# Sliding-window attention and MLP, two layers on one core: score tiles of 64 keys, and the output product of two head groups in one burst

## The chip, the cores and the metric

The kernel runs on one core of a Trainium2 chip. The metric is the device time of one execution in microseconds (us), the median of several. A profile of one execution gives the start and length of every instruction on the five engines: TensorE (PE; its weight loads are listed apart, as PEld), VectorE (DVE), ScalarE (ACT), GpSimd (POOL) and SyncE (SP), which here only issues transfers.

## What is computed

Two layers over 2048 tokens of width 576; each is attention in a sliding window, then an MLP, both after a layer norm and added to the input:

```python
def _A_ref(x, wqkv, wo):
    B, S, D = x.shape
    H = 32; Dh = D // H; W = 256
    qkv = (x @ wqkv).reshape(B, S, 3, H, Dh).transpose(2, 0, 3, 1, 4)
    q, k, v = qkv[0], qkv[1], qkv[2]
    scores = einsum("bhqd,bhkd->bhqk", q, k) * (Dh ** -0.5)
    mask = (idx[:, None] - idx[None, :] >= 0) & (idx[:, None] - idx[None, :] < W)
    p = softmax(where(mask, scores, -1e9))
    o = einsum("bhqk,bhkd->bhqd", p, v)
    return o.transpose(0, 2, 1, 3).reshape(B, S, D) @ wo

def _B_ref(x, w1, b1, w2, b2):
    h = gelu(einsum("bsd,df->bsf", layernorm(x), w1) + b1)      # 576 -> 4608
    return einsum("bsf,fd->bsd", h, w2) + b2                    # 4608 -> 576

for layer in range(2):          # the same weights in both
    x = x + _A_ref(layernorm(x), A_wqkv, A_wo)
    x = x + _B_ref(layernorm(x), B_w1, B_b1, B_w2, B_b2)
```

32 heads have 18 elements each. A query sees itself and the 255 keys before it, so a block of 128 keys is seen by three blocks of 128 queries: its own (where the upper triangle is masked), the next (all of it), and the one after (where the other triangle is masked).

## The kernel before

**Who sets the order.** Python code describes every piece of work as a task with its engine, what it reads and writes, a cost and a priority (`Plan.add`, L206). `Plan.schedule` (L257) plays these through engine by engine and always takes the task that can start first, ties by priority; it also assigns the eight PSUM banks, and puts dummy matmuls (`warm_fn`, L604) into planned gaps of TensorE in the first 140 us. The order so found is written out, one in-order stream an engine, and `Sched.add` (L65) puts in the semaphore waits. TensorE never waits for its own earlier work there (L75, L82). `PL.nudge` (L463) is a table of numbers that are added to the priorities of named stages; `FEED_UNTIL` (L418) is the time until which the planner holds TensorE work back that would make ACT run dry.

**How the work is cut.** Tokens stand in 16 tiles of 128 a layer, four tiles to a chunk: eight chunks, k = 0 to 7, of which 0 and 4 start a layer. Heads stand in eight groups of four. The main loop (L1032) mixes, for every k, the attention of chunk k (`E`, L858), the MLP of chunk k-1 (`G_part` for the first product and gelu, `mm2` for the second), the projections of chunk k+1 (`qkv`, L718), and the output projection with residual and layer norm (`tail`, L886).

**Attention of one group.** The four heads of a group lie on the partitions 0, 32, 64, 96. `scores` (L777) has keys on the output partitions: the matmul at L789 takes 32 rows (one head's dimensions, padded) and 128 keys, so the array works as four tiles of 32x128 side by side, one for a head. The 128-key blocks of a chunk are packed into three units (`units_of`, L765); in an inner chunk each has 512 columns of queries, in the first chunk of a layer 384, 512 and 256. A unit fills two pairs of PSUM banks (`SC`). ACT takes the exponential of each pair into `pT` (L798), and POOL sets the masked triangles to zero with an affine select over all 128 partitions (L819). `pv` (L824) multiplies by the values: tiles of 128x32, four heads side by side, 18 value columns and a one that gives the softmax sum (L834), all three units of a group in one burst of 24 matmuls into one bank, one unit behind the last scores. DVE transposes the result, divides by the sum, and transposes again for the output projection (L845 to L855).

**The MLP.** `G_part` adds the last 64 of the 576 rows for six column blocks at once, in two tiles of 64x128 (L919), which takes six banks; then four matmuls of 128 rows each (L931), gelu on ACT (L934). `mm2` has 288 columns a matmul (L960) and takes a bank of `FILL` (7, 6, 5, 4). Score and MLP banks overlap (`SC` uses 0 to 5, `MM1` all).

**The start.** SP loads the token tiles into `x_in` (the buffer of `w2`), ACT's queue loads the qkv weights (`w_load`, L573), then ACT loads its table of functions (L988). DVE clears the four upper banks (L601), computes statistics and normalizes; the first four tiles are transposed by TensorE (L657).

**Layer norm in the tail.** The last 64 columns of a normalized tile are written twice (for the two 64-row tiles), the second time by a second DVE instruction (L648, `dup`); SP then issues a transposing transfer (L663).

## Time and profile before

| | |
|---|---|
| median of three runs | 895.23 us (895.12 to 896.53) |
| the profiled execution | 897.23 us, its span 895.5 us |
| first matmul | 9.13 us |
| score matmuls L789, units | 1216, 192 |
| output product L834, bursts | 1408, 64 |
| exp L798 | 384 instructions, 345.8 us busy on ACT |
| masks L819 | 368 instructions, 283.5 us busy on POOL |
| mm2 L960, L931, qkv and output projection L699 | 2304, 1152, 1280 matmuls |

"x" with a number is a count of instructions. Names stand as output<-input with shapes as partitions x elements. In a timeline, equal instructions in a row are merged: the first number is their start, the second the time from the first start to the last end. A bracket tells how long the engine was idle before and what ended that. A matmul's record is longer than the time that it occupies the array: the next one starts while it still drains.

### The profile page before, as it was taken

What the parts mean: (1) busy time and instruction counts of PE and PEld (TensorE: products, weight loads), DVE (VectorE), ACT (ScalarE), POOL (GpSimd) and SP (SyncE); (2) the same over time, 40 slices, a digit from 0 to 9 for tenths busy, and PEclk for the clock granted to TensorE, in tenths of its full rate; (3) what the DMA queues carried; (4) which work ended last, traced back from release to release, by engine and by line L of the source; (5) the groups of instructions that cost most, each with busy time, mean ns of one, the idle gap of its engine ahead of it and who ended that gap; (6) DMA issues with size and microseconds to landing.
All of it is one profiled execution on the core that took longest, in us unless ns stands there. A gap on an engine that the chain in (4) does not pass through costs nothing.

```text
span 895.5 us, 19577 instructions
## 1 busy us (share of the span) xinstructions
PE 864.4 (97%) x7849; PEld 506.5 (57%) x7901; DVE 410.1 (46%) x969; ACT 615.8 (69%) x737; POOL 366.2 (41%) x504
## 2 busy tenths in 40 slices
PE   5898999999999999999999999999999999999998
PEld 4555455656566565665655655556556545556665
DVE  6789223863357351763427633375134523161111
ACT  3976888577767788366773868747777689844443
POOL 3677544274244662224431544416444266231100
PEclk9999999999999999999999999999999999999999
DMA  6788537742477333853457342682537632446431
GB/s 177 139 172 173 179 119 182 178 109 81 149 166 158 120 120 98 183 124 121 130 119 181 71 158 86 143 198 67 165 119 147 184 125 71 144 126 176 153 96 50
DMA packets 182649, 122.25 MB, mean 137 GB/s; under 512 B 107424, under 2 KB 181024, under 8 KB 182560
## 3 DMA queue, kind: packets, MB, share of 16 engines
q1 hardware_dynamic: 179152, 115.47, 49.5%
q0 software_dynamic: 1584, 3.54, 1.5%
q10 hardware_dynamic: 1824, 1.99, 0.7%
q8 instruction: 63, 1.03, 0.5%
q14 instruction: 26, 0.21, 0.1%
HBM read 91.28 MB, written 2.36 MB: 105 GB/s over the span
## 4 chain that ended last, share of the span: by engine, by line
PE 54%; DVE 1%; issue 1%; DMA 1%; ACT 1%; POOL 0%
PE ps L960 21%; PE ps L931 18%; PE ps L699 6%; PE ps L789 3%; PE ps L919 3%; PE ps L834 3%; ACT pT L798 1%; DVE x_res L880 0%; DMA xnTa<-xn 0%; DVE st_all L620 0%; DMA xnTm<-xn 0%; DVE xn L643 0%; DVE xn L648 0%; POOL rstd L633 0%; DVE xn L883 0%
## 5 line engine op out<-in xcount | busy, mean ns | idle before, releaser
L819 POOL TENSOR_SCALAR_AFFINE_SELECT pT<-pT 128x512 bf16<-128x512 bf16 (+1 forms) x368 | 283.5, 794 | 266.6 <-ACT pT L798 262.0
L798 ACT ACTIVATE pT<-ps 128x1024 bf16<-128x1024 f32 (+2 forms) x384 | 345.8, 972 | 58.3 <-PE ps L789 57.8
L934 ACT ACTIVATE hT<-ps,b1col 128x512 bf16<-128x512 f32 x288 | 197.8, 687 | 192.8 <-PE ps L931 188.3
L960 PE MATMUL ps<-w_sb,hT 128*128 128x288 bf16 x2304 | 309.5, 287 | 0.2
L960 PEld LDWEIGHTS ps<-w_sb,hT 128*128 128x128 bf16 x2304 | 213.9, 98 | 81.9 <-issue 24.9
L931 PE MATMUL ps<-xnTm,w_sb 128*128 128x512 bf16 x1100 | 255.0, 380 | 4.9 <-issue 3.2
L931 PEld LDWEIGHTS ps<-xnTm,w_sb 128*128 128x128 bf16 x1152 | 109.6, 98 | 137.0 <-issue 19.1
L880 DVE TENSOR_TENSOR x_res<-ps,x_res 128x288 f32<-128x288 f32 x216 | 95.9, 448 | 169.0 <-PE ps L960 158.4
L699 PE MATMUL ps<-wqkv,xnTa 128*128 128x288 bf16 x960 | 136.0, 289 | 3.5 <-DVE qn L742 1.9
L845 DVE STREAM_TRANSPOSE oq<-ps 128x512 f32<-128x512 f32 x64 | 45.8, 715 | 179.0 <-PE ps L834 178.8
L699 PEld LDWEIGHTS ps<-wqkv,xnTa 128*128 128x128 bf16 x960 | 88.4, 98 | 41.4 <-issue 7.8
L742 DVE CAST qn<-ps 128x288 bf16<-128x288 f32 x120 | 53.2, 449 | 35.1 <-PE ps L699 33.0
L942 POOL TENSOR_TENSOR x_res<-x_res,b2bc 128x576 f32<-128x576 f32 x32 | 40.8, 1274 | 69.2 <-ACT hT L934 69.2
L789 PE MATMUL ps<-qT,kT 32*128 32x384 bf16 (+2 forms) x1216 | 64.1, 276 | 2.2 <-ACT pT L798 2.0
L631 POOL TENSOR_SCALAR vtmp<-mv_all 128x1 f32<-128x1 f32 (+1 forms) x43 | 8.5, 197 | 121.4 <-DVE mv_all L622 120.6
L834 PE MATMUL ps<-pT,vA 128*20 128x384 bf16 (+2 forms) x1408 | 50.7, 276 | 2.0 <-ACT pT L798 0.9
L620 DVE BATCH_NORM_STATS2 st_all<-x_res 128x6 f32<-128x288 f32 x104 | 44.8, 448 | 1.2
L919 PE MATMUL ps<-xnTm,w_sb 64*128 64x512 bf16 x288 | 39.7, 381 | 5.5 <-ACT pT L798 3.3
L789 PEld LDWEIGHTS ps<-qT,kT 32*128 32x128 bf16 x1216 | 19.5, 92 | 44.1 <-issue 25.1
L699 PE MATMUL ps<-wo_sb,attT 128*128 128x288 bf16 x320 | 42.8, 286 | 0.1
L834 PEld LDWEIGHTS ps<-pT,vA 128*20 128x20 bf16 x1408 | 25.7, 90 | 26.8 <-issue 13.4
L729 DVE CAST vA<-ps 128x288 bf16<-128x288 f32 x64 | 28.8, 454 | 23.7 <-PE ps L699 23.4
(47 smaller groups left out, 347.6 us busy)
## 6 DMA issues: line engine op xcount, KB each, us to landing
w_sb<-in_B_w_dram SPq DMA_DIRECT2D x48, 864.0 KB, 5.4
w_sb<-in_B_w_dram SPq DMA_DIRECT2D x48, 768.0 KB, 4.7
w_sb<-in_B_w_dram SPq DMA_DIRECT2D x96, 48.0 KB, 4.4
x_res<-in_A_x_dram POOLq DMA_DIRECT2D x3, 1152.0 KB, 7.0
out_dram<-xn SPq DMA_DIRECT2D x16, 144.0 KB, 1.8
wqkv<-in_A_wqkv_dram ACTq DMA_DIRECT2D x3, 576.0 KB, 6.9
w_sb<-in_A_x_dram SPq DMA_DIRECT2D x2, 576.0 KB, 4.2
wo_sb<-in_A_wo_dram SPq DMA_DIRECT2D x4, 144.0 KB, 2.6
```

Source lines behind the costliest of these rows:

```text
L699: ins = e.matmul(bank(bs[o])[:, 0:HB], lhs(c), rhs(c, o * HB), start=(c == 0), stop=(c == KD - 1))
L742: add("dve", lambda e, b=bs[o], dst=dst: e.tensor_copy(dst, heads_of(bank(b))), reads=[bs[o]], writes=[f"qn{sl}h{o}"], cost=0.375, lat=0.1 ...
L789: ins = e.matmul(two(bs[j // 2])[:, j % 2, col:col + nq * 128], k_of(T0 + so)[0][32 * j:32 * j + 32, g, :], qs[32 * j:32 * j + 32, g, qo * ...
L798: add("act", lambda e, h2=h2: e.activation(pT[:, sl, 2 * h2:2 * h2 + 2, lo:hi], two(bs[h2])[:, :, lo:hi], ACT.Exp, scale=SCALE), reads=[bs ...
L819: add("pool", lambda e, ap=ap, pat=pat, sgn=sgn, kind=kind: e.affine_select(ap, ap, pattern=pat, compare_op=(ALU.is_ge if kind == "d" else ...
L834: ins = e.matmul(bank(bo)[32 * j:32 * j + VW, qo * 128:(qo + nq) * 128], vA[:, (T0 + so) % VS, 8 * j + g, :], pT[:, sl, j, col:col + nq * ...
L845: add("dve", lambda e: e.transpose(oq[:, 0:4 * nt, :].rearrange("p b c -> p (b c)"), bank(bo)[:, 0:nt * 128]), reads=[bo, f"aq{(g - 1) % G ...
L880: add("dve", lambda e: e.tensor_tensor(x_res[:, t, sl], bank(b)[:, 0:HB], x_old[:, t, sl], ALU.add), reads=[b] + ([f"xin{t}"] if first els ...
L919: ins = e.matmul(bank(bk)[:, 0:n], w1_sb[64 * b:64 * b + 64, sl, col:col + 128], xnTm[64 * b:64 * b + 64, k % 2, 4, 0:n], start=True, stop ...
L931: ins = e.matmul(bank(bk)[:, 0:n], w1_sb[:, sl, col:col + 128], xnTm[:, k % 2, c, 0:n], start=False, stop=(c == 3))
L934: add("act", lambda e, ff=ff, fl=fl, bk=bk: e.activation(hT[:, fl, 0:n], bank(bk)[:, 0:n], ACT.Gelu_apprx_tanh, bias=b1col[:, ff:ff + 1]), ...
L960: ins = e.matmul(bank(b)[:, 0:HB], hT[:, fl, i * 128:(i + 1) * 128], w2_sb[:, fl, hh * HB:(hh + 1) * HB], start=(fl == 0), stop=(fl == NFH ...
```

## The change

1. **Score tiles of 64 keys.** A block of 128 keys is scored as two halves of 64 (tiles of 32x64, eight side by side). For each half only the 320 queries that see any of its keys are computed, not 384, and the columns start at the half's first query. Units have 512, 320 and 448 columns in an inner chunk, and 320, 448 and 256 in a layer's first. `pT` becomes three buffers of unit kind 0, three of kind 1 and two of kind 2.
2. **Masks.** Blocks are 64 queries wide. POOL masks the diagonals of the lower half (64 partitions), of the upper half (128 partitions), and the far edge of the lower half; the far edge of the upper half is a minimum with a constant mask on DVE, which is made at the start.
3. **Output product.** `pv` takes two groups at once, each with its own bank, in tiles of 64x32: in phase 0 the upper keys of the second group run beside the lower keys of the first, in phase 1 the other way round. Phase 1 waits for the semaphore of phase 0 (`own=True`). There are 32 bursts of two phases.
4. **The start.** The table load of ACT stands ahead of its weight transfers. The four upper banks are cleared by TensorE with dummy matmuls (`clear`), not by DVE; more dummy matmuls fit in before the first tile. The load of tiles 8 to 11 waits for `q2`, not `k3`; `b1in` lies in `hT`.
5. **The rest.** The second copy of the last 64 columns goes from DVE to POOL; five buffers `qn`, not six; other bank choices for some tasks; `FEED_UNTIL` is 0; finer stage names in chunks 0, 1 and 7 (`FINE`), and a new table of nudges. `DRV = -1` and `DRQ = 0` leave the split between ACT and DVE as it was.

```diff
-            if lw is not None and not (eng == "pe" and lw[2] == "pe"):
+            if lw is not None and (own or not (eng == "pe" and lw[2] == "pe")):
...
-FEED_UNTIL = 40.0
+FEED_UNTIL = 0.0
...
-    PS = 6
-    PVG = [()] * 8
-    PVLAG = 1
+    PR = (3, 3, 2)
+    UW = (512, 320, 448)
+    LAG = 2
...
-    NQN = 6
+    NQN = 5
...
+    add("act", lambda e: e.preload_act_table_set("exp_and_others"), cost=1.4, lat=0.0, fifo="act", plain=True, prio=-10)
     w_load(0)
...
-    for i in OUT:
-        b = Bank((i,))
-        add("dve", lambda e, b=b: e.memset(bank(b), 0.0), writes=[b], cost=0.56, lat=0.1, prio=-7, alloc=[b])
...
+    add("dve", lambda e: e.tensor_copy(mk[64:128, :], unit(0, 0)[64:128, 0, 64:128]), reads=["p0_0m0"], writes=["mask"], cost=0.09, prio=-7)
...
+    for i in OUT:
+        b = Bank((i,))
+
+        def clear(e, b=b):
+            for h in range(2):
+                ins = e.matmul(bank(b)[:, 256 * h:256 * h + 256], warm[:, 0:128], warm[:, :], start=True, stop=True)
+            return ins
+        add("pe", clear, reads=["warm"], writes=[b], cost=0.45, lat=0.2, prio=-7, alloc=[b])
...
         if dup:
-            add("dve", lambda e: e.tensor_scalar(xn[:, sl, D:KD * 128], s[:, t, 512:D], mv_all[:, t, 0:1], rstd[:, t:t + 1],
-                                                  op0=ALU.subtract, op1=ALU.mult),
+            add("pool", lambda e: e.tensor_copy(xn[:, sl, D:KD * 128], xn[:, sl, 512:D]), reads=[f"xn{sl}"], writes=[f"xd{sl}"], cost=0.33,
...
         if nt == 4:
-            us = [[(0, 0, 3, 0), (-2, 0, 1, 384)], [(1, 1, 3, 128), (3, 3, 1, 0)], [(-1, 0, 2, 0), (2, 2, 2, 256)]]
+            us = [(1, [0]), (2, [1, 3]), (0, [2])] if t0 == 0 else [(0, [0, -2, 3]), (1, [1]), (2, [-1, 2])]
...
+                for b in range(2):
+                    lo = 128 * max(so, 0) + (64 * b if so >= 0 else 0)
+                    hi = 128 * min(so + 3, nt) - (64 * (1 - b) if so + 3 <= nt else 0)
+                    pad = 64 * b if even else 0
+                    halves.append((lo, hi, at[b] + pad, pad))
+                    at[b] += hi - lo + pad
...
-                    ins = e.matmul(two(bs[j // 2])[:, j % 2, col:col + nq * 128], k_of(T0 + so)[0][32 * j:32 * j + 32, g, :],
-                                   qs[32 * j:32 * j + 32, g, qo * 128:(qo + nq) * 128], start=True, stop=True, tile_position=(32 * j, 0))
+                        ins = e.matmul(two(bs[j // 2])[64 * b:64 * b + 64, j % 2, col:col + hi - lo],
+                                       k_of(T0 + so)[0][32 * j:32 * j + 32, g, 64 * b:64 * b + 64],
+                                       qs[32 * j:32 * j + 32, g, lo:hi], start=True, stop=True, tile_position=(32 * j, 64 * b))
...
+                add("dve", lambda e, ap=ap, mo=mo: e.tensor_tensor(ap, ap, mo, ALU.min),
+                    reads=[f"p{sl}h0", f"p{sl}h1", "mask"], writes=[f"p{sl}m{mi}"], cost=0.06 + 0.27 * nb, lat=0.14, prio=prio)
...
+        def fn(e, ph):
+            ins = None
+            at = [0, 0]
+            got = []
+            for b, i in ((1, 1 - ph), (0, ph)):
+                for x in half(i, b):
+                    got.append((at[b], len(got), x))
+                    at[b] += x[4] - x[3]
+            seq = [x[2] for x in sorted(got, key=lambda x: x[:2])]
...
+                    ins = e.matmul(bank(bo[i])[32 * j:32 * j + VW, lo:hi], vA[64 * b:64 * b + 64, (T0 + so) % VS, 8 * j + gs[i], :],
+                                   pu[64 * b:64 * b + 64, j, col:col + hi - lo], start=(ph == 0 and i not in begun),
+                                   stop=(ph == 1 and not any(x[0] == i for x in seq[n + 1:])), tile_position=(64 * b, 32 * j), skip_group_check=True)
...
+        for ph in range(2):
+            ncol = max(sum(x[4] - x[3] for x in half(ph, 0)), sum(x[4] - x[3] for x in half(1 - ph, 1)))
+            add("pe", lambda e, ph=ph: fn(e, ph), reads=rd, writes=bo, cost=0.02 + 0.1 * ph + ncol * 0.000425, prio=prio - 0.1 * ph, lat=0.2, mode="c",
+                alloc=(bo if ph == 0 else ()), fifo="pv", own=(ph == 1))
...
-    table("exp", -10)
...
-    xin_load(8, 4, ["k3"], -4)
+    xin_load(8, 4, [GX], -4)
```

## The prediction

> **What bounds the kernel now.** I read the page's busy times and its chain first, then a table by stages, then the timeline of one attention stage and of the first 18 us, and last the groups by shape.
>
> ```profile
> PE 864.4 (97%) x7849; PEld 506.5 (57%) x7901; DVE 410.1 (46%) x969; ACT 615.8 (69%) x737; POOL 366.2 (41%) x504
> ...
> PE 54%; DVE 1%; issue 1%; DMA 1%; ACT 1%; POOL 0%
> ```
>
> TensorE is busy for 97% of the span, and the chain that ended last names hardly anything but TensorE lines. So a change is worth what it takes from TensorE's stream, unless some stage has another limit. The stages show two that have (columns: stretch, its length, then busy us of PE, PEld, DVE, ACT and POOL, granted clock, DMA):
>
> ```profile
> 22.00:50.00 28.00, 24.48 (x281) 13.90 (x281) 22.72 (x59) 25.50 (x37) 19.27 (x27) 1.00 0.79 150
> 50.00:80.00 30.00, 29.53 (x342) 18.51 (x342) 26.22 (x60) 20.85 (x26) 20.13 (x30) 1.00 0.94 198
> 80.00:92.00 12.00, 9.34 (x114) 5.26 (x106) 11.84 (x29) 9.74 (x11) 10.08 (x15) 1.00 0.37 72
> ...
> 600.00:716.00 116.00, 115.47 (x1087) 67.82 (x1095) 48.17 (x110) 85.95 (x99) 48.11 (x64) 1.00 0.52 137
> 716.00:745.00 29.00, 26.80 (x257) 13.44 (x262) 7.71 (x16) 24.01 (x29) 16.05 (x19) 0.94 0.41 129
> 745.00:806.00 61.00, 57.82 (x554) 32.69 (x558) 25.48 (x61) 45.09 (x53) 26.23 (x38) 1.00 0.35 110
> ```
>
> In 600 to 716 us PE idles 0.5 us of 116; the stages from 92 us on that I don't show are alike. From 22 to 92 us it idles 6.7 of 70 us, and VectorE is busy 60.8 of them. From 716 to 806 us it idles 5.4 us, and 6% of the clock is missing in 29 us, another 1.7 us.
>
> ```profile
> 319.70 0.12 PEld L789 LDWEIGHTS ps<-qT,kT 32*128 32x128 bf16 x8 [0.24 <-issue]
> ...
> 320.04 1.64 PE L960 MATMUL ps<-w_sb,hT 128*128 128x288 bf16 x12
> ...
> 321.61 0.12 PEld L789 LDWEIGHTS ps<-qT,kT 32*128 32x128 bf16 x8 [0.24 <-issue]
> ...
> 323.54 0.83 PE L834 MATMUL ps<-pT,vA 128*20 128x384 bf16 x24
> ...
> 326.94 0.40 PE L789 MATMUL ps<-qT,kT 32*128 32x256 bf16 x8
> ...
> 327.39 7.51 ACT L798 ACTIVATE pT<-ps 128x1024 bf16<-128x1024 f32 x8 [0.70 <-PE ps L789]
> ```
>
> Here is the price of a short burst. From one score unit's weight loads (319.70) to the next (321.61) are 1.91 us: one unit of 512 columns and 12 matmuls of L960. The 12 run in 1.64 us, the last record lasting 0.287, so one takes (1.64-0.287)/11 = 0.123 us, 0.427 ns a column. 1.91 - 1.476 - 512 x 0.000427 leaves 0.215 us for two changes of tile shape, 0.11 each.
>
> **The change, term by term (profiled execution: 897.23 us, 1.7 of it outside the span of 895.5; the median of the runs is 895.23. The terms are differences, and I apply their sum to the median.)**
>
> *Columns.* The masked halves of blocks are no longer computed. A group had 512+512+512 columns in the six inner chunks (48 groups) and 384+512+256 in the two that start a layer (16); now 512+320+448 and 320+448+256. That is 48 x 256 + 16 x 128 = 14,336 columns less for the scores, and as many for the output product: 2 x 14,336 x 0.427 ns = -12.2 us, if eight tiles stream beside each other as four do now.
>
> *Changes of shape.* The instruction order of the built kernels has 551 changes before and 520 after: -31 x 0.11 = -3.4 us.
>
> *The boundary in each output burst.* The second of its two phases waits for the semaphore of the first (`own=True`), 32 times; the matmuls queued behind it, and the mm2 and qkv work after them, all wait. No row has PE waiting for itself. Nearest: exp starts 0.05 us after the modelled end of its scores (327.39 after 326.94+0.40), and the record of a 128-column score matmul lasts 214 ns, 0.16 more than its columns. So 0.21 each, +6.7 us. Bounds: 0.11 (a change of shape), 3.5 us; 0.42 (the idle time by issue before L931's loads), 13.4 us.
>
> *Start of a burst.* The eight loads above start within 0.12-0.09 = 0.03 us, 4 ns apart. With eight tiles instead of four the last begins 16 ns later: 256 bursts, +4.1 us; bounds 0 and twice that.
>
> *Short parts.* The burst at 323.54 takes 0.83-0.273 = 0.56 us from first to last start, the columns before the last part (1280) 0.547: loads hide behind parts of 128 columns (55 ns). New are 208 parts of 64 columns (27 ns). If a load needs the 55, each waits 28 ns: 5.8 us at most, 0 at least. The two halves run beside each other, so I take +1.5. The Trainium skill (TensorEngine Tiling (Array Packing), Feature Incompatibilities) says column tiling gives up the fast weight load, which speaks against 64-column score tiles. This trace's column-tiled loads (L834, mean 90 ns for 20 columns, 98 for the plain ones) show no loss, but none is 64 wide. By TensorE: Matmul & The Clock Gate (LDWEIGHTS), 64/1.2 gives an estimate of 53 ns for such a load, by which this term would be near its upper end.
>
> TensorE in sum: -12.2 - 3.4 + 6.7 + 4.1 + 1.5 = **-3.3 us**, between -12.1 and +11.8.
>
> *Other engines.*
>
> ```profile
> L798 ACT ACTIVATE pT<-ps 128x1024 bf16<-128x1024 f32 x320 | 305.5, 1025 | 48.5 <-PE ps L789 48.2
> ...
> L819 POOL TENSOR_SCALAR_AFFINE_SELECT pT<-pT 128x512 bf16<-128x512 bf16 x256 | 162.5, 650 | 215.3 <-ACT pT L798 212.6 <-PE ps L960 0.2 <-PE ps L919 0.2
> ...
> L819 POOL TENSOR_SCALAR_AFFINE_SELECT pT<-pT 128x1024 bf16<-128x1024 bf16 x112 | 126.0, 1125 | 51.2 <-ACT pT L798 49.4
> ...
> L919 PE MATMUL ps<-xnTm,w_sb 64*128 64x512 bf16 x288 | 39.7, 381 | 5.5 <-ACT pT L798 3.3 <-DVE xn L643 1.0 <-DMA xnTm<-xn 0.4
> ...
> L798 ACT ACTIVATE pT<-ps 128x512 bf16<-128x512 f32 x32 | 17.5, 609 | 4.5 <-PE ps L789 4.5
> ```
>
> Exp: 1025 and 609 ns give 0.81 ns a column, so 713 for 640 and 921 for 896. Per inner group 2 x (1025+713+921) instead of 6 x 1025, per first group 2 x (713+921+609) instead of 2 x (810+1025+609): 373 us of records become 327. Nothing of that is on the path where PE is full. POOL: 0.93 ns a column gives 0.41 us for 256; 10 x 0.41 + 0.65 = 4.8 us a group stays as it is (4 x 0.65 + 2 x 1.125), +3 in all, and 32 copies of 64 columns (0.26, the memset of `xn`) +8: 43% busy, its idle time covers it. The copy stands behind masks in POOL's queue and ahead of the transpose on SP's; that counts only where the first and last MLP wait for it, some 0.3 us each. DVE gains a mask of 512 columns (0.72, as L845) and two of 256 (0.40, between L648's 308 ns and L851's 458) per inner group, two of 256 per first group: +86 -12 for the dropped copies, 410 to 484 us, 55%. From a pair's last score unit to its output burst the order has 4.2 us of TensorE work in the median (lowest 2.35; before 3.8 and 2.3); the exps and masks need 0.25+2x0.92+3x0.41 = 3.3 against 0.25+2x1.025+2x0.65 = 3.6. So the cover still holds, and I put 0; without it the waits would be 0.5 us at some ten bursts.
>
> *22 to 92 us.* Before the first MLP part DVE gets 22 masks (20 x 0.40 + 2 x 0.72), five casts more (2.3), and loses four copies (1.5) and two turns of the output (2.2): +8 on 60.8 of 70 us. ACT does 5.7 us less here. DVE would be full; I take **+2**, between -3 and +8.
>
> *The first 15 us.*
>
> ```profile
> 4.44 1.28 ACT L975 ACT_TABLE_LOAD   x1 [4.44 <-issue]
> 4.75 0.76 DVE L620 BATCH_NORM_STATS2 st_all<-w_sb 128x6 f32<-128x288 bf16 x2
> ...
> 10.72 1.39 PE L699 MATMUL ps<-wqkv,xnTa 128*128 128x288 bf16 x5
> ...
> 12.44 4.42 PE L699 MATMUL ps<-wqkv,xnTa 128*128 128x288 bf16 x25
> ...
> 17.14 3.84 PE L699 MATMUL ps<-wqkv,xnTa 128*128 128x288 bf16 x30
> ```
>
> 25 matmuls of L699 take 4.42 us at 12.44 and 30 of them 3.84 at 17.14: 0.172 against 0.122 each, and the first five take 1.39 where five take 0.79 later. TensorE is slow there by 1.2+0.6 = 1.8 us. After, 41 dummy matmuls of 256 columns stand ahead (8 that clear PSUM, 33 to keep busy), from 1.1 us to 5.6 at full rate or 10.1 at half, 1.0 too late in that case. The rows are slow until TensorE has worked about 5 us (9.13 to 15) and full from then on; the dummies are that much work, so I take the whole 1.8 as won. The Trainium skill (TensorE: Matmul & The Clock Gate, Part 1) has the clock at half until about 3.4 us of sustained work; the two rates above agree with it, and by it the dummies end before the first tile is ready. Four PSUM memsets (2.11 us) no longer stand before the first tile's statistics (4.75), and the table load (1.28) now stands ahead of the weight loads on ACT's queue, so the token tiles land first; up to 1.1 us earlier, but weights may be late by the 1.28. I take -1.8-0.7 = **-2.5**, between -2.9 and +1.3.
>
> *716 to 806 us.* L919 waits 3.3 us for exps that hold its banks, and the slow clock follows the longest such wait. Exps are shorter and the order there is new: half of 5.4+1.7, **-3.5**, between -7 and +3. Fewer `qn` buffers, `b1in` in `hT`, and the load of tiles 8 to 11 one transpose earlier (-0 to 0.5) I put at 0: the buffers have 92 us or transposes before them.
>
> Sum: -3.3+2-2.5-3.5 = -7.3; 895.23-7.3 = **888 us**.
>
> **Rivals.** (1) *The array packs cleanly*: boundary 0.11, no spread, no short-part wait. PE -12.1, the rest as above: 879. For it: four tiles pack to 13 ns now. Against: a wait on a semaphore is more than a change of shape. Chance 0.14. (2) *Burst overheads eat the columns*, the other side: boundary 0.42, twice the spread, short parts 1.5: PE +7.5 and 895.2+7.5-4 = 899; it decides once PE's sum is above +4. For it: the 0.42 of L931; against: exps see 0.05. Chance 0.14. (3) *Two column tiles of one row strip don't stream together*: the scores' 77,824 columns run twice, +33: 921. Against: L834's four column tiles do stream together now; 0.04. (4) *VectorE bounds the early stage*: +8 there and the late waits only move (0): 895.2-3.3+8-2.5 = 897; for it 60.8 of 70; 0.06. (5) *Nothing moves*: the late waits and early idle grow by what PE saves, 895; 0.07. That the change isn't what it says is excluded by the order: the columns and changes counted are those of the built kernel.
>
> **Numbers.** Forecast 0.55, its own range 880 to 893. Downward the term spreads are 8.8, 5, 0.4 and 3.5, in quadrature 11; upward 15, 6, 4 and 6.5, 18. Ends of 875 and 903 leave out half of rival 3's side and little else, about 0.2 in all. 0.2% is 1.8 us, what a measurement here can tell. Faster: 0.54 of the forecast and 0.14: 0.68. Slower: 0.14+0.04+0.04 of rival 4: 0.22. Same: 0.10.
>
> **What would show it.** Right: score units of 0.22, 0.14 and 0.19 us of columns, and 0.21 more for two changes; output phases of 0.55 with a gap near 0.2; PE idle not above 10 us of the stretch from 92 to 716 (6.4 now); L724's first 30 at 0.122 each. Wrong: a score burst as long as before; gaps inside bursts at 64-column parts; DVE over 95% from 22 to 92 us with PE idle over 10; output bursts waiting for POOL or DVE masks.

## The result and the profile after

| | median of the runs (us) | lowest to highest | profiled execution, its span |
|---|---|---|---|
| before | 895.17 | 894.57 to 896.53 | 897.23, 895.5 |
| after | 904.46 | 901.51 to 907.46 | 906.29, 904.3 |

The ratio is 1.0104, 95% interval 1.0075 to 1.0132: 9.3 us slower, where 7.3 us less were forecast. A second set of runs of the same kernel (e8 below) gives 903.15 and 1.0093 (1.0070 to 1.0115).

From the page of after, the busy times and the chain:

```profile
PE 876.9 (97%) x10801; PEld 530.3 (59%) x10801; DVE 473.7 (52%) x1111; ACT 570.6 (63%) x737; POOL 385.9 (43%) x856
...
PE 82%; DMA 7%; DVE 5%; ACT 2%; issue 1%; POOL 1%; SPq 0%; ACTq 0%; DVEq 0%; POOLq 0%
```

TensorE is as full as before by this line, and yet the chain names other engines for 15% of the span. Part of TensorE's busy time is now dummy matmuls in places where it has nothing to do (51 of them behind the first tile's transposes, where the kernel before has 8). The two chains don't cover the same stretch, though: that of before, followed back, ends at 380 us, so its 58% say nothing of the early stage; that of after reaches the start. The table by stages (the same columns as in the prediction):

```profile
22.00:50.00 28.00, 26.16 (x423) 16.82 (x415) 24.14 (x62) 19.55 (x29) 18.98 (x46) 1.00 0.70 141
50.00:80.00 30.00, 26.95 (x472) 16.43 (x464) 25.10 (x60) 21.29 (x30) 20.59 (x49) 1.00 0.93 176
80.00:97.00 17.00, 12.60 (x243) 8.77 (x245) 15.86 (x39) 9.64 (x12) 13.89 (x34) 1.00 0.54 110
...
600.00:716.00 116.00, 113.26 (x1419) 67.44 (x1418) 58.09 (x132) 74.27 (x94) 48.13 (x104) 0.99 0.53 138
716.00:745.00 29.00, 28.23 (x398) 16.78 (x396) 16.69 (x38) 22.58 (x28) 19.23 (x44) 1.00 0.50 136
745.00:806.00 61.00, 58.20 (x840) 33.40 (x840) 22.81 (x50) 46.41 (x60) 26.98 (x58) 1.00 0.33 104
```

The early stage (its end, the first MLP part, moved from 92.47 to 96.85 us) leaves TensorE idle for 9.3 of 75 us (22 to 97), plus the dummies. The stage from 600 to 716 idles 2.7 us where it idled 0.5. Only from 716 to 806 it is better: idle 3.6 instead of 5.4 us, and the clock is whole.

**What the attention costs on TensorE now.** Weight loads (PEld) of after, the same view as the one the prediction priced a short burst from:

```profile
326.01 0.16 PEld L834 LDWEIGHTS ps<-qT,kT 32*64 32x64 bf16 x16 [0.24 <-ACT pT L843]
326.34 1.34 PEld L1052 LDWEIGHTS ps<-w_sb,hT 128*128 128x128 bf16 x12 [0.17 <-issue]
327.92 0.29 PEld L834 LDWEIGHTS ps<-qT,kT 32*64 32x64 bf16 x24 [0.24 <-issue]
328.27 1.34 PEld L1052 LDWEIGHTS ps<-w_sb,hT 128*128 128x128 bf16 x12
329.85 0.12 PEld L834 LDWEIGHTS ps<-qT,kT 32*64 32x64 bf16 x8 [0.24 <-issue]
330.12 0.60 PEld L1052 LDWEIGHTS ps<-w_sb,hT 128*128 128x128 bf16 x6
330.96 0.54 PEld L914 LDWEIGHTS ps<-pT,vA 64*20 64x20 bf16 x48 [0.24 <-issue]
331.81 0.53 PEld L914 LDWEIGHTS ps<-pT,vA 64*20 64x20 bf16 x48 [0.31 <-PE ps L914]
332.48 0.16 PEld L834 LDWEIGHTS ps<-qT,kT 32*64 32x64 bf16 x16
332.80 2.08 PEld L1052 LDWEIGHTS ps<-w_sb,hT 128*128 128x128 bf16 x18 [0.17 <-issue]
```

The unit of 448 columns (16 loads at 326.01) takes 1.91 us with its 12 matmuls of L1052, as much as 512 columns took before; the one of 512 takes 1.93, the one of 320 1.11 with six. The 0.31 on the eighth line is the boundary: the second phase's loads wait for TensorE's own semaphore. In the starts of the matmuls there are 0.265 us more between the phases than columns. Over all undisturbed bursts the medians, changes of shape included, are 0.370, 0.426 and 0.455 us for units of 320, 448 and 512 columns (before 0.319, 0.372 and 0.428 for 256, 384 and 512; 256 columns now 0.344), and 1.61 us for an inner pair's burst, 1.35 for one of the first chunk (before 0.862 and 0.697 for each single one). Summed over the 64 groups: scores -1.6 + 0.3, output 38.6 + 10.8 - 41.4 - 11.2 = -3.1, together **-4.4 us**. TensorE's price in undisturbed bursts fell about as forecast (-3.3). (L789 before has 1408 matmuls; the 1216 in the table of before leave out 192 whose keys lie in `x_res`.)

**Where 8.8 us went.** From the first tile's transposes (9.13 and 9.12 us) to the last matmul there are 883.0 us before and 891.9 after. Of the difference, by the starts of all matmuls: attention bursts -4.4; dummies in gaps after the start +4.6 (8 matmuls before, 51 after, 0.107 us each); waits over 0.3 us +4.1 (14.5 to 18.7); TensorE at half clock +1.7 (one stretch of 3.4 us before, two after); the rest, waits under 0.3 us, +2.8. So waits ate the saving, with the dummies that fill some of them, and the first question is what the largest ones wait for.

VectorE at the end of chunk 0's attention, before (one group's output) and after (a pair's). A turn is the transpose of one group's output and what follows it up to `attq`:

```profile
68.54 0.72 DVE L845 STREAM_TRANSPOSE oq<-ps 128x512 f32<-128x512 f32 x1 [0.16 <-PE ps L834]
69.29 0.25 DVE L848 RECIPROCAL rinv<-oq 128x16 f32<-128x16 f32 x1
...
69.95 0.45 DVE L851 TENSOR_TENSOR attq<-oq,rinv 128x288 bf16<-128x288 f32 x1
...
70.68 1.29 DVE L855 STREAM_TRANSPOSE attT<-attq 128x512 bf16<-128x512 bf16 x2
```

```profile
73.55 0.72 DVE L931 STREAM_TRANSPOSE oq<-ps 128x512 f32<-128x512 f32 x1
...
74.78 0.67 DVE L937 TENSOR_TENSOR attq<-oq,rinv 128x288 bf16<-128x288 f32 x1
75.48 0.38 DVE L878 TENSOR_TENSOR pT<-pT,mk 64x256 bf16<-64x256 bf16 x1
75.89 0.72 DVE L931 STREAM_TRANSPOSE oq<-ps 128x512 f32<-128x512 f32 x1
76.53 0.42 DVE L772 CAST qn<-ps 128x288 bf16<-128x288 f32 x1
...
78.35 1.31 DVE L941 STREAM_TRANSPOSE attT<-attq 128x512 bf16<-128x512 bf16 x2
```

Before, the last output of chunk 0 is in `attT` at 71.97 us, 3.4 us after its turn began; after, at 79.66, 6.1 us after the first of two turns began, with masks and casts between. Of these 7.7 us, 2.7 are the turns and 0.9 the longer burst ahead of them. The other 4.2 us were late already: chunk 0's last score unit starts at 68.5 instead of 64.4, its last output burst at 71.97 instead of 67.82. From there the chain goes on: output projection from 80.06 (72.87 before), residual, statistics, GpSimd's `rstd`, normalization, the copy of the last columns, one transpose a tile in SP's queue, first MLP part. The last of those transposes left SP at 94.93 us (90.75) and landed at 96.34 (92.12), and the part began 0.50 us behind the landing (0.35):

```profile
92.47 0.82 PE L919 MATMUL ps<-xnTm,w_sb 64*128 64x512 bf16 x6 [0.41 <-DMA xnTm<-xn]
```

That is the line of before; the one of after stands with e2 below. Of the 7.7 us only 4.4 arrive at the first MLP part: from `attT` to there it takes 17.2 us where it took 20.5. Much of the lateness is in the written order. By the times that `Plan.schedule` itself assigns, chunk 0's last score unit comes at 66.05 instead of 62.64 us, and the first MLP part at 92.21 instead of 89.86.

The waits of TensorE from 92 to 716 us (us in total, times, longest), after and before:

```profile
PE ps L724 <- DMA xnTa<-xn: 3.6, 4, 1.3
PE ps L1011 <- DVE oq L931: 2.2, 1, 2.2
PE ps L834 <- DMA xnTm<-xn: 0.9, 1, 0.9
```

```profile
PE ps L699 <- DMA xnTa<-xn: 0.5, 1, 0.5
```

The 2.2 us of L1011 (L919 before) are the wait at the end of the early stage. Behind it the new waits are for token tiles: qkv of the next chunk stands ready to start before its tile is normalized and transposed. From the first MLP part to the last matmul's start there are 804.1 us after and 799.7 before, so in this execution the loss is split evenly between the early stage and what follows it.

### The profile page after: what moved, and what is told of

The parts are those of the page before. It is cut to its first block, busy times and chain, and to the rows that moved or that the text cites. A ratio compares the mean times of both kernels' runs of the same rounds, so it can differ in the third digit from the quotient of the medians.

```text
span 904.3 us, 25747 instructions
## 1 busy us (share of the span) xinstructions
PE 876.9 (97%) x10801; PEld 530.3 (59%) x10801; DVE 473.7 (52%) x1111; ACT 570.6 (63%) x737; POOL 385.9 (43%) x856
## 4 chain that ended last, share of the span: by engine, by line
PE 82%; DMA 7%; DVE 5%; ACT 2%; issue 1%; POOL 1%; SPq 0%; ACTq 0%; DVEq 0%; POOLq 0%
PE ps L1052 30%; PE ps L1023 26%; PE ps L724 13%; PE ps L834 5%; PE ps L914 4%; PE ps L1011 4%; DMA xnTa<-xn 2%; ACT pT L843 2%; DMA w_sb<-in_A_x_dram 2%; DVE st_all L646 1%; DMA qT<-qn 1%; DMA x_res<-in_A_x_dram 1%; POOL pT L881 1%; DVE pT L878 1%; DVE x_res L970 1%
## 5 line engine op out<-in xcount | busy, mean ns | idle before, releaser
L881 POOL TENSOR_SCALAR_AFFINE_SELECT pT<-pT 128x256 bf16<-128x256 bf16 (+1 forms) x688 | 296.2, 464 | 244.2 <-ACT pT L843 243.7
L843 ACT ACTIVATE pT<-ps 128x640 bf16<-128x640 f32 (+3 forms) x384 | 300.3, 846 | 112.7 <-PE ps L834 111.8
L1052 PE MATMUL ps<-w_sb,hT 128*128 128x288 bf16 x2304 | 309.4, 287 | 0.2
L1023 PE MATMUL ps<-xnTm,w_sb 128*128 128x512 bf16 x1152 | 264.5, 381 | 0.0
L1052 PEld LDWEIGHTS ps<-w_sb,hT 128*128 128x128 bf16 x2304 | 214.4, 98 | 71.7 <-issue 8.2
L878 DVE TENSOR_TENSOR pT<-pT,mk 64x256 bf16<-64x256 bf16 x176 | 78.6, 447 | 30.0 <-ACT pT L843 24.7
L834 PE MATMUL ps<-qT,kT 32*64 32x320 bf16 (+4 forms) x2432 | 63.7, 268 | 3.2 <-ACT pT L843 1.8
L834 PEld LDWEIGHTS ps<-qT,kT 32*64 32x64 bf16 x2432 | 29.2, 103 | 44.2 <-issue 22.7
L914 PE MATMUL ps<-pT,vA 64*20 64x320 bf16 (+4 forms) x2816 | 45.6, 255 | 4.3 <-ACT pT L843 1.1
L1011 PE MATMUL ps<-xnTm,w_sb 64*128 64x512 bf16 x288 | 39.6, 380 | 4.1 <-DVE oq L931 2.2
L914 PEld LDWEIGHTS ps<-pT,vA 64*20 64x20 bf16 x2816 | 30.3, 85 | 22.5 <-PE ps L914 9.9
```

Source lines behind the costliest of these rows:

```text
L834: ins = e.matmul(two(bs[j // 2])[64 * b:64 * b + 64, j % 2, col:col + hi - lo], k_of(T0 + so)[0][32 * j:32 * j + 32, g, 64 * b:64 * b + 64 ...
L843: add("act", lambda e, h2=h2: e.activation(pu[:, 2 * h2:2 * h2 + 2, lo:hi], two(bs[h2])[:, :, lo:hi], ACT.Exp, scale=SCALE), reads=[bs[h2] ...
L878: add("dve", lambda e, ap=ap, mo=mo: e.tensor_tensor(ap, ap, mo, ALU.min), reads=[f"p{sl}h0", f"p{sl}h1", "mask"], writes=[f"p{sl}m{mi}"], ...
L881: add("pool", lambda e, ap=ap, pat=pat, sgn=sgn, b=b: e.affine_select(ap, ap, pattern=pat, compare_op=(ALU.is_ge if sgn == 1 else ALU.is_g ...
L914: ins = e.matmul(bank(bo[i])[32 * j:32 * j + VW, lo:hi], vA[64 * b:64 * b + 64, (T0 + so) % VS, 8 * j + gs[i], :], pu[64 * b:64 * b + 64, ...
L1011: ins = e.matmul(bank(bk)[:, 0:n], w1_sb[64 * b:64 * b + 64, sl, col:col + 128], xnTm[64 * b:64 * b + 64, k % 2, 4, 0:n], start=True, stop ...
```

## The experiments

All are the changed kernel unless another is named; each ratio is against the kernel before, run on the same chip beside it.

**e1, e5, e6: the masks.** Rival 4 of the prediction. These kernels leave three quarters of the masking out (e5: of VectorE's alone).

```
-add("dve", lambda e, ap=ap, mo=mo: e.tensor_tensor(ap, ap, mo, ALU.min),
+add("dve", lambda e, ap=ap[:, 0:1], mo=mo[:, 0:1]: e.tensor_tensor(ap, ap, mo, ALU.min),
-add("pool", lambda e, ap=ap, pat=pat, ...: e.affine_select(
+add("pool", lambda e, ap=ap[:, 0:1], pat=[[0, 1]] + pat[1:], ...: e.affine_select(
```

> Every mask, on VectorE and on GpSimd, covers the columns of one of the four heads instead of all four (three quarters of the masking are left out); the order on each engine and every wait stay. Theory W (TensorE's own price of the attention fell by about 4 us as forecast, and waits ate it: the stage from 22 to 97 us is set by VectorE's and GpSimd's queues, which the masks fill): the first MLP part, at 96.85 us now, starts 2 to 5 us earlier; its wait of 2.2 us becomes short enough that the half clock behind it (97.4 to 100.8 us, worth 1.7) is gone; in all 4 to 7 us less than the 904.5, so 898 to 900. Rival B (the boundaries inside the output bursts eat the columns; masks are covered everywhere): within 1 us of 904.5.

> As in e1, but only VectorE's masks are shortened to one head (its far-edge masks of three heads of four are left out); GpSimd's stay whole; same order. e1 gained 3.7 us (900.75 against 904.46) and its first MLP part began 1.8 us earlier. If VectorE's queue is what holds the early stage (it stands in the way of the output's turns and the casts): 2.5 us or more of that, 902 or less, first MLP part at least 1.2 us earlier than 96.85. If GpSimd's masks hold it: under 1.2 us, 903.5 or more.

> The kernel before with its masks shortened to one head of four in the same way (three quarters of the masking are left out); same order. A control for e1: if what masks hold up is new with the change, this gains at most 1.5 us on 895.4. If masks cost the kernel before as much as the changed one, it gains 3 us or more, and masks explain none of the difference.

Measured: e1 900.75 us, ratio 1.0057 (1.0041 to 1.0073), first MLP part at 95.07. e5 901.46, 1.0075 (1.0052 to 1.0098), at 95.77. The control e6, on the kernel before: 891.86 against 894.66, 0.9969 (0.9955 to 0.9983), its first MLP part at 89.09 instead of 92.47. So shorter masks help the changed kernel by about 3.7 us (2.4 against its second set of runs, e8) and the kernel before by 2.8: masks are in the way of both, and explain about 1 us of the difference at most. In the early stage they explain none: with short masks the first MLP part of the changed kernel comes 6.0 us after that of the kernel before, with whole ones 4.4. VectorE's masks are most of what e1 gained (3.0 of 3.7 us), but e5's first MLP part came 1.08 us earlier and not the 1.2 expected. Without e6, e1 would have passed for the answer.

**e2: the clock.**

```
-n = int((b - a - 0.1) * 0.8 / 0.115)
+n = int((b - a - 0.1) * 0.8 / 0.115) + (20 if 89.0 < a < 89.1 else 0)
```

> 20 more dummy matmuls (2.1 us at full clock) behind the 21 that stand ahead of the first MLP part, where TensorE waits 2.24 us now. If the clock halves from 97.42 to 100.8 us because TensorE stood idle just before, it stays full, L1023 runs there at 0.213 us a matmul instead of up to 0.43, and the second part of that stage starts 1.5 to 1.9 us earlier than 104.53, in all -1.7 us. If the clock falls for another cause: no change. If the dummies last longer than the wait: up to 0.3 us later.

TensorE around the first MLP part in after, and in e2:

```profile
92.21 2.47 PE L625 MATMUL ps<-warm 128*128 128x256 bf16 x21
96.85 0.94 PE L1011 MATMUL ps<-xnTm,w_sb 64*128 64x512 bf16 x6 [2.17 <-DVE oq L931]
97.72 6.44 PE L1023 MATMUL ps<-xnTm,w_sb 128*128 128x512 bf16 x22
```

```profile
94.39 4.65 PE L625 MATMUL ps<-warm 128*128 128x256 bf16 x41
98.97 0.82 PE L1011 MATMUL ps<-xnTm,w_sb 64*128 64x512 bf16 x6
99.95 5.13 PE L1023 MATMUL ps<-xnTm,w_sb 128*128 128x512 bf16 x23 [0.16 <-issue]
```

With the gap filled the matmuls behind it run at full rate (5.13 us for 23, not 6.44 for 22), and the second part follows the first after 6.04 us instead of 7.68: a half clock there goes with the wait, and costs 1.64 us. But the last transpose here left SP only at 96.45 us and landed at 97.86 (96.34 in after); the part began 1.11 us behind it, behind the dummies, and not the 0.41 that is usual: they were 0.7 us too long. And the clock had halved already, ahead of them (the columns are those of the table by stages, the clock is the last but two):

```profile
90.90:94.31 3.41, 2.90 (x112) 1.56 (x112) 2.31 (x5) 0.95 (x2) 3.34 (x9) 0.50 0.77 75
```

So this run moved the half clock and did not remove it. The median is 906.31, 1.0121 (1.0101 to 1.0142), no gain.

**e3 and e12: the boundary.** e12 is e3 and e9 together.

```
+def swap(order):
+    pe = [n for n, x in enumerate(order) if x[1].eng == "pe"]
+    for a, b in [(a, b) for a, b in zip(pe, pe[1:]) if order[a][1].own and order[b][1].mode == "r"]:
+        order.insert(b, order.pop(a))
+    return order
```

> Where a score unit follows a pair's output burst on TensorE (22 of 32), that unit is put between the burst's two phases; nothing else of the order changes. The traced boundary is 0.265 us with nothing in it; the unit in between makes one change of shape more (0.1). Rival B and theory W agree on the price here if the gap is a plain wait: 22 x (0.265 - 0.1) = -3.6 us, and no gap of 0.26 inside those bursts any more. If the gap is not a wait on the first phase's end but a price of starting 64-row tiles in crossed halves, it stays in the trace, and the time is the same or 2 us longer. If the later end of the second phase delays VectorE's turn of the output where that is what ends the early stage: -2 only.

> e3 and e9 together on the changed kernel: the score unit between the phases of 22 bursts and the two turns of a pair ahead of the masks between them. If the two prices are separate, their gains add: -3.6 and -2 to -3.5 against 903.2 to 904.5, so 897 to 899, 2 to 4 us above before. If the later phases take back what the turns gain: 900 or more.

The same pair's burst in e3 as in the loads shown above:

```profile
328.95 0.54 PEld L914 LDWEIGHTS ps<-pT,vA 64*20 64x20 bf16 x48 [0.24 <-issue]
329.63 0.16 PEld L834 LDWEIGHTS ps<-qT,kT 32*64 32x64 bf16 x16
329.96 0.53 PEld L914 LDWEIGHTS ps<-pT,vA 64*20 64x20 bf16 x48 [0.17 <-PE ps L914]
330.63 2.07 PEld L1052 LDWEIGHTS ps<-w_sb,hT 128*128 128x128 bf16 x18
```

Pair and unit take 1.68 us to the next load of L1052, 1.84 in after: 0.16 less. 16 of the 22 filled bursts gain 0.14 to 0.17 us in this way. So the boundary is a plain wait. In three the unit between has to wait itself by about 0.1 us and the gain is nil; three more lose 0.15 to 0.34. By the starts all 22 together gain about 1.9 us, half of the 3.6 expected. The median is 903.05, 1.0081 (1.0065 to 1.0097): 1.4 us under the first set of runs, and as long as e8's 903.15. In the profiled execution two waits near 764 us let the clock fall, which they didn't in after. e12: 903.69, 1.0085 (1.0066 to 1.0104), no better than either alone.

**e4: one weight load.** The w1 load at 601 us brings a quarter (`nc4 = 1 if B == 31 else 4` rows of 128).

> The w1 load issued at 601 us (768 KB, between the first two transposes of MLP token tiles) brings a quarter of its rows; three quarters are left out, so one block of the first MLP matrix is the previous one. Theory W, form 1 (at 609.5 to 612.4 us TensorE waits 2.4 us for token tiles whose transposes share the DMA engines with that load, and the half clock from 612.8 to 616.3 follows from the wait): the four transposes behind the load take 1.3 us each instead of 1.7 to 2.3, the waits fall to under 1 us, the half clock is gone, -2 to -4 us. Form 2 (the chain of residual, statistics, normalization and one transpose queue is late whatever the load does): the waits stay within 0.5 us, same time.

906.62, 1.0112 (1.0092 to 1.0131); the waits near 611 us, by the starts 0.98 and 1.40 in after, are 0.98 and 1.25. Form 2: the load isn't it.

**e7 and f2: the start alone.**

```
-add("dve", lambda e, b=b: e.memset(bank(b), 0.0), writes=[b], ...)
+add("pe", clear, reads=["warm"], writes=[b], ...)
...
-table("exp", -10)
+add("act", ... preload_act_table_set("exp_and_others") ...)   # ahead of w_load(0)
```

> The kernel before with three things of the change's start and nothing else: the table load first on ScalarE, the upper banks cleared by dummy matmuls, and so more dummies before the first tile. The order of all other instructions is that of before. By the prediction's term for the first 15 us: -1.8 (the first 30 qkv matmuls at 0.122 us each instead of up to 0.172) and up to -0.7 for earlier tiles, so 892.9 to 893.6. If the waits behind the first tiles take it back: 895.

> f1 with the change's start (table load first, banks cleared by dummies), as in e7. e7's first MLP part came 1.3 us earlier (91.15 against 92.47) though its median did not: if that is real, f1 less 1.3, and faster than the kernel before by 1 to 6; if late waits take it back as in e7, f1's time within 1.

e7's first MLP part comes at 91.15, 1.3 us earlier, and keeps that to 497 us, where a wait of 2.0 us for a token tile takes it back; its profile ends 1.6 us earlier all the same, because the half clock near 728 us didn't come, but the median is 896.01, 1.0015 (1.0002 to 1.0029). f2 (f1, explained below, with this start) is at 899.02, 1.0039 (1.0025 to 1.0053), f1 without the start at 899.19.

**e8: the changed kernel again.**

> The changed kernel once more, unchanged, on the chip of the three others, so that e1 to e5 have a value of their own day to stand against: 904.5 +- 2; the wait ahead of the first MLP part again over 2 us with the half clock behind it, and the two waits near 610 us again.

903.15. Its profiled execution is its shortest (span 899.8): the half clock fell on the dummies, and none came near 612. The first MLP part is at 96.88, and from there to the last matmul it takes 799.5 us, as before (799.7). In this execution the whole loss is in the early stage; but that of before, longer than any of its five runs above, lost 1.7 us to a half clock near 728 in this stretch, so the saving of the tiles is gone there too.

**e9, f4, f6: what ends the early stage.** e9 moves VectorE's masks behind a pair's second turn; f4 is e9 without the 21 dummies (`n = 0 if 89.0 < a < 89.1`), f6 is e9 with 12 dummies and the last two tiles' steps on GpSimd ahead of three masks.

```
+def turns(order):
+    for a in [n for n, x in enumerate(order) if x[1].writes == ("oq",)][::2]:
+        b = next(n for n in range(a + 1, len(order)) if order[n][1].writes == ("oq",))
+        m = [x for x in order[a:b] if x[1].eng == "dve" and "m" in str(x[1].writes[0])[3:]]
+        order[a:b + 1] = [x for x in order[a:b + 1] if x not in m] + m
+    return order
```

> On VectorE, far-edge masks that stand between a pair's two turns of the output go behind the second turn (23 places in its queue differ, all else is the same). Theory P (a pair holds two banks and its turns follow one another, so VectorE has to pass the first group's turn and the masks in between before the second bank comes free for the first MLP part): the wait of 2.2 us ahead of the first MLP part shrinks to under 1 us, it starts 1.5 to 2 us earlier than 96.85, the half clock behind it cannot follow; the median falls by 2 to 3.5 us from 903.2 to 904.5. If the part waits for ScalarE or for token tiles instead: under 0.5 us.

> e9 without the 21 dummies ahead of the first MLP part (there they took 3.9 us at a low clock and ended at 96.57, after the bank of the pair's second group came free at 95.28). If that bank ends the stage: the first MLP part starts at 95.3 to 95.5. If the last token tile does (its duplicate columns stood behind GpSimd's masks until 93.1, then one transpose): 95.7 to 96.4. The clock then falls behind the wait: no gain in the median over 1 us, 901.5 to 903.5.

> e9 with the last two token tiles' steps on GpSimd ahead of the three masks of the next pair that stood between them, and 12 dummies instead of 21 ahead of the first MLP part. e9 and f4 freed the bank at 95.3 and 96.1 and the part began at 96.6 and 97.6, about 1 us behind the last transfer of a token tile. If the early stage of the changed kernel ends with these two chains together: the first MLP part at 95.2 to 96.0 (a start like e9's), median 1 to 2 below 903.2. If a third chain ends there: no earlier than 96.5.

The second turn's transpose, which frees the bank, ended at 96.76 in after, 95.28 in e9, 96.05 in f4 and 95.69 in f6; the first MLP part began at 96.85, 96.64, 97.63 and 97.59. What goes with it is the last token tile (times from the records of SP and of its transfer):

```
            last transpose issued    landed    first MLP part    behind landing
before        89.55 to 90.75         92.12         92.47             0.35
after         93.71 to 94.93         96.34         96.85             0.50
e8            93.29 to 95.02         96.47         96.88             0.41
e9            93.19 to 94.76         96.23         96.64             0.41
f4            93.96 to 95.70         97.12         97.63             0.51
f6            93.50 to 95.73         97.18         97.59             0.41
```

In 18 of the 20 traces the part begins 0.35 to 0.51 us behind this landing (e2: 1.11, the dummies; e11: 0.99). In after the bank came free within 0.1 us of that moment, which is why the view of waits could name VectorE's `oq`; with the bank free 1.4 to 1.9 us ahead of the part (e9, f4, f6), the part still waits for the token tile. So theory P is wrong: the bank is not what ends the stage. In f6 the copy of the last columns came 1.0 us earlier than in f4 and the transpose then took 2.23 us to issue instead of 1.74; why transposes here take 1.2 to 2.6 us to issue isn't shown. Medians: e9 902.73 (1.0080, 1.0062 to 1.0098), f4 907.25 (1.0129, 1.0110 to 1.0148), f6 905.25 (1.0108, 1.0082 to 1.0134) where 899.7 to 902.5 (theory P), 901.5 to 903.5 and 901.2 to 902.2 were expected.

**e10, e11, f5: is it the order?** The planner of the changed kernel takes score units and output bursts for cheaper than traced. e10 gives it the traced prices (also +0.05 for GpSimd's masks), e3's rule and a new table of nudges:

```
-cost=0.01 + ncol * 0.00042, ...            # a score unit
+cost=0.046 + ncol * 0.00042, ...
-cost=0.02 + 0.1 * ph + ncol * 0.000425, ...   # a phase of an output burst
+cost=0.02 + 0.02 * ph + ncol * 0.000425, ...  # and 0.27 more where nothing stands between the phases
```

e11 and f5 are the kernel before (e11 with the start of e7, f5 unchanged up to 133 us) with another table of nudges.

> The changed kernel with the planner's prices of score units (+0.036 us each), output bursts (+0.27 for a boundary with nothing in it) and GpSimd masks (+0.05) set to those traced, the rule of e3 in the planner, and a new table of nudges found by its own model with these prices. Its plan ends at 895.96 us; the plan of before ended at 889.50 and ran 895.5. Theory W (the waits come with the pairs, the masks and the shorter cover, whatever the order): plan plus 6, so 900 to 904, no better than the changed kernel by more than 3. Rival O (only the order is at fault, planned with prices that the chip doesn't have): 895 or less.

> The kernel of e7 (before with the change's start) with a new table of nudges from the same search as e10. Its plan ends at 886.53, 3.0 earlier than before's. If the search is as good as the one behind the tables there: 892 +- 2, faster than before. If a new order costs what it gains: 895. It is the control for e10: the same search on both.

> Control for f1: the kernel before, instruction for instruction, its order unchanged up to 133 us, and behind that a table of nudges found anew by the same search from none. Its plan ends at 887.9, 1.6 earlier than before's 889.5. If f1's loss of 3.2 us is the order's (any table that the chip has not been asked about meets token tiles that land late): 897 to 901. If it is the tiling's: 893 to 896, no slower than the kernel before.

e10: 906.93, 1.0130 (1.0105 to 1.0156), above what either theory expected. As its plan, at the traced prices, ends at 895.96, this doesn't show that no better order exists. e11: 900.48, 1.0048 (1.0031 to 1.0065), though its plan is 3 us shorter than that of the kernel before; e7, with the same start, is 1.4 us over the kernel before, e11 4.8. Its first MLP part is at 97.78, planned for 88.31. The longest of TensorE's waits from 9 to 98 us there:

```profile
PE ps L704 <- DMA xnTa<-xn: 4.5, 2, 2.6
```

f5: 897.81, 1.0020 (1.0008 to 1.0033). So an order that a plan calls better costs 2 us in the middle of the very kernel before, and 3.4 us over e7 when it is new from the start. The waits that come with it in e11 are for token tiles, which land later than that order needs them.

**f1 and f3: the new tiling in the middle only.** The kernel before, with the change's tiles, bursts and masks where `k in NEW` (2 to 6; in f3 2 to 7), buffers of exps (3, 2, 2), e3's rule, and a new table of nudges from 144 us on.

```
 def E(k, gs, prio):
+    if k in NEW:
+        return E2(k, gs, prio)
```

> The kernel before, its start and its order up to 144 us unchanged, with the change's score tiles, paired output bursts, masks and e3's rule in chunks 2 to 6 alone (three, two and two buffers of exps, a pair's burst at most one score unit late), traced prices in the planner, and a new table from the same search. Its plan ends at 889.49, as before's did, with the score units priced as traced here. Theory S (the tiling pays as forecast where TensorE is full, 20 pairs at -0.18 and some 15 filled boundaries at -0.17, about -6 us of TensorE; what the change lost, it lost in the first 97 us and in the waits at the two ends): 890 to 896, and the first MLP part at 92.5. Theory M (the middle loses by itself: pairs shorten the cover, each new wait halves the clock): 898 or more, with waits of over 1 us between 145 and 716.

> f1 with chunk 7 in the new tiling too, with a table from the same search; plan 892.22, 2.7 more than f1's. By the plan 893 to 898, 2 to 4 above f1, with the waits at the end of chunk 7's attention (745 to 806 us). If the last chunk gains as the prediction had it (-3.5 for 716 to 806): not slower than f1.

f1: 899.19, 1.0036 (1.0022 to 1.0050); f3: 899.73, 1.0047 (1.0031 to 1.0064). Chunk 0's last output in f1, and its first MLP part:

```profile
69.72 1.29 DVE L891 STREAM_TRANSPOSE attT<-attq 128x512 bf16<-128x512 bf16 x2
```

```profile
91.39 0.82 PE L1134 MATMUL ps<-xnTm,w_sb 64*128 64x512 bf16 x6 [0.21 <-DVE qn L778]
```

With chunks 0 and 1 as before, `attT` is done at 71.01 and the early stage ends at 91.39: its loss is gone, and some 5 of the 8 to 9 us with it. (Chunks 0 and 1 have the old tiles, the old bursts and the old order here; the run doesn't tell these apart.) The middle neither pays nor loses much: f1 is 3.2 us over the kernel before, f5, whose middle is only ordered anew, 2, and their intervals overlap. f3, with chunk 7 too, is the same as f1 within the noise. Theory S was right about the early stage and wrong about the gain.

## Why the prediction was wrong

Two steps of the sum failed. The end of the early stage came 4.9 us later than forecast, and from there to the last matmul, where the forecast had about -6.8 us (-3.5, and most of the -3.3), the profiled executions show +4.4 (after) and -0.2 (e8). The prediction had read "the chain that ended last" as TensorE's through and through; that chain begins at 380 us, behind the early stage.

- **TensorE sum, -3.3.** Right in size: -4.4 in the trace's undisturbed bursts. Within it, *boundary* was 0.265 each and not 0.21 (+8.5), the *start of a burst* as said (the second half's tiles start 13 to 23 ns behind the first), and *short parts* too small and put in the wrong place: in every unit of two or more parts the first change of part waits 27 ns for its load, be it 192 columns or 320 (part of 192 columns: 80 ns, the next starts at 107). With it, 448 columns cost what 512 did. The Trainium skill (TensorEngine Tiling (Array Packing), Feature Incompatibilities) says that column tiling gives up the fast weight load; the 27 ns agree with loads that no longer hide, and no run here shows the load's mode.
- **22 to 92 us, +2.** This is the first step that failed. The end of the stage was due at 92.0 by the forecast (92.47 + 2 - 2.5) and came at 96.85; with the 1.96 us that the start had won, the stage lost 6.3 us. I counted VectorE's work (+8 on 60.8 of 70 us), and not the chain that ends the stage. In the trace a chunk whose output comes by pairs has it in `attT` 3.5 us later from the start of its last burst (2.7 of them in the turns), and the tiles of the first MLP part follow from there. That the loss sits in chunks 0 and 1 is shown by f1; that the pairs cause it is argued from this timeline and not shown. VectorE wasn't full (65.1 of 75 us), and e1, e5 and e6 show masks to explain none of the stage's lateness, so rival 4 had the right stage and the wrong mechanism.
- **The cover, 0.** This is the second. "From a pair's last score unit to its output burst" it held: output bursts wait for masks in no line above. The wait went elsewhere, to the next chunk's token tiles (from 0.5 to 4.5 us in the view of waits), for which I had no term, and to many waits under 0.3 us (+2.8 in all).
- **The first 15 us, -2.5.** The rates came as said (25 qkv matmuls in 3.23 us), and the next 30 began at 15.18 instead of 17.14. The tiles weren't ready earlier in after's profile (9.12 against 9.13); e7 shows 1.3 us at the first MLP part and nothing in the median.
- **716 to 806 us, -3.5.** Right in this execution: 1.8 us less idle and 1.7 us of clock. The clock's part is partly luck: e3, f6 and e10 have a half clock in this stage.
- **Not priced for new waits:** that a wait drags the clock down behind it, though the prediction saw it at 728 us. The Trainium skill (TensorE: Matmul & The Clock Gate, Part 1) lets the clock fall after an idle window of about 3.4 us. Here it fell after 2.17 us of idle time (after, ahead of 97.4 us), and after two waits of 0.91 and 1.31 (after, ahead of 612.8 us); the measurement decides.

What stays open: why chunk 0's last score unit is already 4.1 us late (3.4 of them are in the plan; whether the pairs force them or the table of nudges does: single output bursts with the new score tiles weren't tried), and how much of the middle is due to the tiling beside what any new order costs.

## What to carry to other kernels

Price a change on the fullest engine, and then follow the chain at each place where that engine has no other work: work done by pairs there comes out when the second of the pair is done. Ask of every experiment that helps whether it helps the kernel before as much. And where the order was found by a search, a change brings a new order with it: here that alone moved the time by 2 to 3.4 us, most of the 4 us that the tiles saved.

## What the hardware showed beside that

- TensorE's granted clock changes on a grid. In all 20 traces the stretches at full clock between two half ones are whole multiples of 3.413 us (after: 150 of them from 100.8 to 612.8 us), and a half stretch lasts one such window (two in f4 and f6). What goes with it is TensorE's idle time in the window before: from the clock's first rise to 885 us, each of the 12 full-clock windows with 2.05 us or more of it (by the records of matmuls) was followed by half clock, none with 1.55 or less was, and of those with 1.57 to 1.98 us 12 were and 17 weren't. So a wait counts by how it falls on the grid: 2.26 us in e12, at most 1.85 of them in one window, left the clock whole, and 1.81 us in one window (before, ahead of 728 us) halved it. A half window cost 1.64 us where e2 lets it be compared. The kernel's executions scatter with it: 901.5 (the one at full clock throughout) to 907.5, where the kernel before has 894.6 to 896.5.
- A matmul that waits for TensorE's own semaphore costs 0.265 us of empty time between two phases; 0.14 to 0.17 of it comes back where a score unit that is ready stands between (16 of 22 places).
- Dummies run no faster than the clock they meet: 21 of them took 2.47 us in after, and 3.91 in e9, where the clock had fallen at 92.3 us, ahead of them; there they ended at 96.6 us, when the first MLP part began.
